# Static attention scores in 64-query halves of 192 columns, and dense slots moved forward in the list of slots

## The chip, the cores and the metric

The kernel runs on one core of a Trainium2 chip. The metric is the device time of one execution, in microseconds (us); the median of several runs is given where there are several. A core has five instruction streams that matter here: TensorE (PE in the profile, with its weight loads as PEld), VectorE (DVE), ScalarE (ACT), GpSimd (POOL) and SyncE (SP), which issues the DMAs.

## What is computed

Block-sparse attention over 4 batches, 8 heads, 768 tokens and head dimension 64, followed by a two-layer MLP over the 3072 tokens. All is float32.

```python
def _attn_ref(q, k, v, sampled_blocks):
    block, n_blocks, window = 32, 24, 1
    scores = np.matmul(q, k.transpose(0, 1, 3, 2)) / np.sqrt(D)
    mask = np.abs(blk_i - blk_j) <= window
    mask = mask | (blk_i == 0) | (blk_j == 0) | (blk_i == n_blocks - 1) | (blk_j == n_blocks - 1)
    for qb in range(n_blocks):
        for kb in sampled_blocks[qb]:
            mask[qb * block:(qb + 1) * block, kb * block:(kb + 1) * block] = True
    scores = np.where(mask, scores, -1000000000.0)
    attn = softmax(scores)
    return np.matmul(attn, v)

def _moe_ref(x, w_in, w_out, s, b):
    r = np.maximum(x @ w_in, 0.0)
    return (s * (r * r) + b) @ w_out
```

A token of block i sees blocks i-1, i, i+1, the first and the last block, and three sampled blocks. Tokens of the first and the last block see everything. The MLP has d_model 512 and d_ff 2048; its weights arrive as 64-bit floats that the kernel takes apart by itself.

## The kernel before

**Slots.** Attention is cut into 52 slots, listed in order by the strings under `T["ORD"]` (lines 31 and 32): one string for batches 0 and 1, one for batches 2 and 3, where `a` is the first batch of the pair and `b` the second. `a20` is tile 2, half 0 of the heads. There are three kinds:

- A *tile* slot ("s", 40 of them) handles 128 queries and four heads. Its static scores (`scores_static`, lines 707 to 712) are those of the keys that can be known beforehand: 128 queries times 256 columns of `kt`, one matmul for each head, two heads at a time in the upper and the lower half of the PE rows (`tile_position=(par * D, 0)`). The 256 columns serve two halves of 64 queries, each of which needs only 192. The sampled keys follow (`scores_sampled`, line 736) from `kg`, which POOL has gathered (line 670).
- A *half tile* slot ("h", `aH`, 4 of them) handles the remaining 64 queries of all heads, with 64x64 matmuls of 160 columns in four quarters of the PE (line 724).
- A *dense* slot ("d", `aD0`, 8 of them) handles the queries of the first and the last block against all 768 keys: 64x64 matmuls of 384 columns in four quarters (line 724 too). It needs no gathered keys or values, but twice 384 KB of `v` (line 508).

**Steps of a slot.** Scores go to a PSUM bank; DVE adds the mask and finds the maximum (line 751); ACT takes the exponential (line 763); PE transposes (line 787); DVE and ACT copy the transposes out (lines 791 and 793); PE multiplies with V (lines 821, 832 for the static part, 846 for the sampled); DVE scales (852); PE transposes (858); ACT copies (863); SP spills to DRAM (875). On PE the order is fixed by lines 1025 to 1034: transposes of slot i, the last transposes of slot i-1, scores of slot i+2, V of slot i.

**The weights.** Each of the 32 blocks of weights (16 of `w_in`, 16 of `w_out`, order in `T["WL"]`: i0 to i7, o0 to o6, then both in turn) goes through `decode_f64`: six DVE steps (lines 75, 77, 78, 83, 84, 85) and three ACT steps (79, 81, 82). i0 to i3 are written where the keys of batch 0 (`kt0`) were, i4 to i7 where those of batch 1 were, so step 83 of i0 waits for the last scores of batch 0. A raw block takes one of three `kraw` buffers, and two of these also take the first attention output read back (`xload`, line 359), until `xsplit` (lines 372 and 374) has split it into a `kg` buffer that attention no longer uses.

**The planner.** `Plan` (lines 99 to 198) simulates the engines with costs written by hand (line 956 for PE, lines 993 to 1020 for the others) and puts every operation into its engine's queue in that order; attention goes first, decoding fills what it takes for idle time. The queues are then fixed: on the chip each engine works through its own in order. The first 30 of the MLP's sub-blocks are in the same plan: `mlp1` (lines 401 to 403, weights i) and `mlp2` (lines 440 to 442, weights o). `mlp2` of the first sub-block needs o0. `mlp1` can run ahead of it until the hidden buffers are full.

**Banks.** `next_bank` (line 696) takes a new PSUM tile in one of seven banks in turn for each matrix of scores or transposes; bank 7 holds the outputs.

Of the kernel before, what the change touches and what calls it, by code (L numbers as in the profile page):

```python
# [32 lines left out]
}  # L33


# [63 lines left out]
class Plan:  # L99
# [15 lines left out]
    def op(self, eng, cost, prio, fn, deps=(), alloc=(), use=(), order=(), nbytes=0, cols=0, late=0.0):  # L115


        o = Plan.Op()
        o.cost, o.prio, o.fn, o.nbytes, o.cols, o.late = cost if isinstance(cost, dict) else {eng: cost}, prio, fn, nbytes, cols, late
        o.pick = isinstance(cost, dict)  # L120
        o.deps, o.order, o.alloc = [d for d in deps if d], [d for d in order if d], alloc
        o.end, o.seq = None, len(self.ops)
        for k in (*alloc, *use):
            self.users.setdefault(k, []).append(o)
        self.ops.append(o)
        return o
# [76 lines left out]
def kernel(  # L203
# [16 lines left out]
    nc = tc.nc  # L220
# [3 lines left out]
    D = 64  # L224
# [6 lines left out]
    SC = 256  # L231
# [28 lines left out]
    NBANK = 7  # L260
    RB = 3

    def scratch(tag, n, name):
        return kp.tile([P, KW], F32 if tag == "kraw" else F32R, tag=tag, name=name, bufs=RB if tag == "kraw" else 2)[:, :n]
# [8 lines left out]
    def bank(k, name):  # L273
        return ps.tile([P, 512], F32, tag=f"bank{k}", name=name)
# [87 lines left out]
    def xsplit(g, c, part=None):  # L362
        src = xraw[(g, c // 2)].rearrange("p (t c n) -> p t c n", c=2, n=P)[:, :, c % 2, :]

        def of(k):
            return xsp[(g, k)][:, c, :].rearrange("p (t n) -> p t n", n=P)

        for k in range(2) if part is None else (part,):
            if c == 0:
                xsp[(g, k)] = gp.tile([P, NCC, HALF], F32R, tag="kg", name=f"x{g}_{k}")  # L370
            if k == 0:
                nc.scalar.copy(of(0), src)
            else:
                nc.vector.tensor_tensor(out=of(1), in0=src, in1=of(0).bitcast(F32), op=ALU.subtract)
# [84 lines left out]
    with ExitStack() as es:  # L459
# [12 lines left out]
        slots = []  # L472
        for b0 in range(0, B, 2):
            for w in T["ORD"][b0 // 2].split():
                b, w = b0 + "ab".index(w[0]), w[1:]
                slots.append(("s", b, int(w[0]), int(w[1])) if w[0] in "01234" else (w[0].lower(), b, NSP, int(w[1:] or 0)))
        units = [(i, j) for i, sl in enumerate(slots) for j in range(2 if sl[0] == "d" else 4)]
        unit_of = {}
# [46 lines left out]
        nc.gpsimd.iota(pi, pattern=[[0, 1]], base=0, channel_multiplier=1)  # L525
        for t in ptiles:
            nc.gpsimd.memset(t[:, SW:], 0.0)

        V = nc.vector
        ri = pers.tile([P, 1], I32, name="ri")  # L530
# [163 lines left out]
        bcount = [0]  # L694

        def next_bank(name):
            bcount[0] += 1
            return bank(bcount[0] % NBANK, name)

        halves = [slice(par * D, (par + 1) * D) for par in range(2)]  # L700

        def scores_static(i, k):


            kind, b, t, x = slots[i]
            n, qr, kt = unit_of[i], qraw[slots[i][:3]], kts[b]
            if kind == "s":
                for par in range(2):
                    sp = sps[(n + 2 * k + par, 0)] = next_bank(f"s{n + 2 * k + par}")
                    nc.tensor.matmul(sp[:, :SC], qr[halves[par], 2 * x + k, :], kt[halves[par], 2 * x + k, 192 * t:192 * t + SC],  # L710
                                     start=True, stop=True, tile_position=(par * D, 0))
                return
            for par in range(2):
                key = (n + par, k) if kind == "d" else (n + 2 * k + par, 0)
                sp = sps[key] = next_bank(f"s{key[0]}_{key[1]}")
                for a in range(2):
                    if kind == "d":
                        o = 64 if k else 0
                        keys = kt[halves[par], 2 * x + a, k * 512:k * 512 + 576].rearrange("p (a c) -> p a c", c=192)[:, :, o:o + P]
                        to, q = sp[halves[a], :HALF], qr[halves[par], 2 * x + a, halves[a]]  # L720
                    else:
                        keys, to = kt[halves[par], 2 * k + a, KW - 6 * BLK:KW - BLK], sp[halves[a], SW - SC:2 * P]
                        q = qr[halves[par], 2 * k + a, halves[a]]
                    nc.tensor.matmul(to, q, keys, start=True, stop=True, tile_position=(par * D, a * D))  # L724
# [15 lines left out]
        sps, nms, dns, rcs, tps = {}, {}, {}, {}, {}  # L740
# [42 lines left out]
        def transposes(n, g):  # L783
            src = pbuf[(n, g)]
            tp = tps[(n, g)] = next_bank(f"t{n}_{g}")[:, :3 * P].rearrange("p (c q) -> p c q", c=3)
            for c in range(chunks(n)):
                nc.tensor.transpose(tp[:, c, :], src[:, c * P:(c + 1) * P], ident)  # L787
# [95 lines left out]
        for n, (i, j) in enumerate(units):  # L883
            kind, b, t, x = slots[i]
# [68 lines left out]
        pq = pvl = o_m = o_e = o_rc = o_ev = None  # L953
        spills, tensor, lqs = {}, {}, {}

        costs = {"s": (485, 535, 350, 260, 685), "d": (810, 0, 350, 780, 0), "h": (380, 535, 240, 160, 685)}
        cols = {"s": (1024, 1536, 768, 256, 1024), "d": (1536, 0, 768, 768, 0), "h": (640, 768, 512, 128, 512)}
        for i, (kind, b, t, x) in enumerate(slots):
            u, full, cost, col = unit_of[i], kind == "s", costs[kind], cols[kind]
            nu, ng, nk = (2, 2, 2) if kind == "d" else (4, 1, 2)  # L960
# [14 lines left out]
            for k in range(nk):  # L975
                keys = [(u + par, k) if kind == "d" else (u + 2 * k + par, 0) for par in range(2)]
                o = op("p", cost[0], u, lambda i=i, k=k: scores_static(i, k), cols=col[0],
                       deps=[*(kld[(b, p)] for p in (pairs[k:k + 1] if full else pairs)), lq],
                       alloc=[("B", ("s", *y)) for y in keys], use=[("qr", qk), (f"kt{b}", b)])
                s_ops.append(o)  # L980
                s_of.update((y, [o]) for y in keys)
# [8 lines left out]
            for j in range(nu):  # L990
                n, ms_ = u + j, []
# [55 lines left out]
        for g in range(2):  # L1047
            for c2 in range(2):
# [8 lines left out]
                for c in (2 * c2, 2 * c2 + 1):  # L1057
                    o_x = [xs_ops[(g, 0, 0)]] if c else [xs_ops[(0, 0, 1)]] if g else [pk]
                    xkey = [[("kg", ("x", g, k))] if c == 0 else [] for k in range(2)]
                    h = xs_ops[(g, c, 0)] = op("a", 450, N + T["XP"] + g * 16, lambda g=g, c=c: xsplit(g, c, 0), [xl[(g, c2)]], alloc=xkey[0],  # L1060
                                               use=[key], order=o_x)
# [38 lines left out]
        for k in range(NPL):  # L1100
            g, f = subs[k]
# [6 lines left out]
            if k > 0:  # L1108
                g, f = subs[k - 1]
# [19 lines left out]
    for k, (x, w) in enumerate((("T1", "S1"), ("T3", "S3"), ("T2", "S2"), ("T4", "S4"), ("u", "v"))):  # L1129
        t = scratch("kraw", HX + HN, f"sum{k}") if k < 3 else kp.tile([P, KW], F32, tag="klp", name=f"sum{k}", bufs=2)  # L1130
# [111 lines left out]
    for i in range(NPL, NSUB):  # L1242
        g, f = subs[i]
# [24 lines left out]
    for s in range(S0, B):  # L1268
        a, b = 2 * s, 2 * s + 1
# [114 lines left out]
```

## Time and profile before

| | us |
|---|---|
| median of 3 runs | 809.37 (807.63 to 811.62) |
| the profiled execution | 810.95 |
| its span, first to last instruction | 809.1 |
| PE busy in the span | 785.8 (97%) |
| DVE busy | 566.9 (70%) |
| ACT busy | 493.1 (61%) |
| POOL busy | 144.0 (18%) |

The times are read together: the prediction works on the profiled execution, whose own time is 810.95 us, 1.85 us more than its span. The stages by the trace: start and first loads up to about 33 us, attention up to about 278 us, the 30 planned sub-blocks of the MLP up to about 400 us, then the rest of the MLP. A busy PE is read with care, since the ends of its matmuls are modelled.

### The profile page before, as it was taken

The numbers are of one execution on the slowest core, as the hardware profiler recorded it, in microseconds if no ns is written. First come the engines' busy times: TensorE is split into PE (matmuls) and PEld (weight loads), VectorE is DVE, ScalarE is ACT, GpSimd is POOL, SyncE is SP. The second block draws the span as 40 slices with busy tenths as digits, with TensorE's granted clock in tenths as the row PEclk, the third lists the DMA queues.
The fourth block names the chain that finished last, engine by engine and source line by source line (L and its number), as shares of the span: only waits on it lengthen the run. The fifth ranks groups of instructions, "written<-read, shape, count | busy, mean of one in ns | idle before, by whom it ended". The sixth has DMA issues, their size and how long they took to land.

```text
span 809.1 us, 21895 instructions
## 1 busy us (share of the span) xinstructions
PE 785.8 (97%) x8400; PEld 682.4 (84%) x8400; DVE 566.9 (70%) x1443; ACT 493.1 (61%) x1175; POOL 144.0 (18%) x374
## 2 busy tenths in 40 slices
PE   7899988999999999999999999999999999999997
PEld 6587877888887889999899999998899888899996
DVE  5576767888888998998743333478668769766662
ACT  3576767788788787777673433457345457544542
POOL 5422133222400000000000000003223223322321
PEclk9899999999999999999999999999999999999999
DMA  9999898876777533334230010412200012000002
GB/s 252 242 229 313 237 249 229 240 222 213 207 211 251 145 105 127 106 107 129 85 111 27 29 37 27 157 45 79 85 1 7 0 40 83 16 0 1 1 1 78
DMA packets 86071, 95.60 MB, mean 118 GB/s; under 512 B 11344, under 2 KB 64976, under 8 KB 85968
## 3 DMA queue, kind: packets, MB, share of 16 engines
q1 hardware_dynamic: 85968, 94.21, 38.9%
q8 instruction: 66, 1.08, 0.6%
q14 instruction: 37, 0.30, 0.1%
HBM read 77.41 MB, written 12.58 MB: 111 GB/s over the span
## 4 chain that ended last, share of the span: by engine, by line
PE 86%; DVE 6%; DMA 3%; ACT 2%; issue 2%; SPq 1%; DVEq 0%; ACTq 0%
PE m L1193 13%; PE o L441 10%; PE o L442 10%; PE o L440 10%; PE t L787 8%; PE s L710 5%; PE xs L832 5%; PE h L403 5%; PE h L401 5%; PE h L402 4%; PE xs L846 3%; PE s L736 3%; DMA kt<-in_k_seq_dram 2%; PE s L724 2%; PE xs L858 1%
## 5 line engine op out<-in xcount | busy, mean ns | idle before, releaser
L763 ACT ACTIVATE ptile<-ptile,nm 128x352 f32<-128x352 f32 (+2 forms) x208 | 121.0, 584 | 36.8 <-DVE nm L751 36.5
L1210 ACT ACTIVATE hid<-hid,sb_b,sb_s 128x384 f32<-128x384 f32 x64 | 45.4, 709 | 113.9 <-DVE hid L1204 113.9
L419 POOL TENSOR_TENSOR hid<-hid,hid 128x384 fp32r<-128x384 f32 x64 | 68.7, 1074 | 178.5 <-ACT hid L1211 178.3
L751 DVE CUSTOM_DVE_ANT_0 ptile<-s,ms 128x352 f32<-128x352 f32 x160 | 74.3, 521 | 30.6 <-PE s L736 30.4
L670 POOL COPY kg<-kt 128x128 f32 x264 | 63.6, 293 | 137.3 <-PE s L736 124.0
L401 PE MATMUL h<-x,win 128*128 128x384 f32 x256 | 86.4, 337 | 0.0
L403 PE MATMUL h<-x,win 128*128 128x384 f32 x256 | 86.3, 337 | 0.0
L402 PE MATMUL h<-x,win 128*128 128x384 f32 x256 | 85.9, 336 | 0.0
L787 PE MATMUL t<-ident,ptile 128*128 128x128 f32 x608 | 79.2, 280 | 3.7 <-ACT ptile L763 2.7
L410 DVE SCALAR_TENSOR_TENSOR hid<-hid,sb_s 128x384 f32<-128x384 f32 x64 | 39.5, 617 | 53.8 <-ACT hid L406 53.5
L441 PE MATMUL o<-wout,hid 128*128 128x512 f32 x192 | 76.5, 398 | 0.6 <-DVE wout L85 0.6
L442 PE MATMUL o<-wout,hid 128*128 128x512 f32 x192 | 76.3, 397 | 0.0
L442 PE MATMUL o<-woutr,hid 128*128 128x512 f32 x192 | 75.9, 395 | 0.0
L441 PE MATMUL o<-woutr,hid 128*128 128x512 f32 x192 | 75.8, 395 | 0.0
L440 PE MATMUL o<-wout,hid 128*128 128x512 f32 x192 | 75.2, 391 | 0.0
L440 PE MATMUL o<-woutr,hid 128*128 128x512 f32 x192 | 74.6, 389 | 0.0
L787 PEld LDWEIGHTS t<-ident,ptile 128*128 128x128 f32 x608 | 65.9, 141 | 9.6 <-ACT ptile L763 3.8
L406 ACT ACTIVATE hid<-h 128x384 f32<-128x384 f32 x64 | 31.4, 491 | 69.4 <-PE h L403 69.0
L1179 POOL TENSOR_TENSOR xT<-sum,xT 128x768 fp32r<-128x768 f32 x2 | 3.7, 1853 | 332.2 <-DVE xT L1179 331.1
L1193 PE MATMUL m<-xT,wop 128*128 128x384 f32 x288 | 58.9, 338 | 2.6 <-DVE sum L1286 1.5
L791 DVE COPY pt<-t 128x384 f32<-128x384 f32 (+1 forms) x104 | 56.1, 543 | 7.6 <-PE t L787 6.1
L419 DVE TENSOR_TENSOR hid<-hid,hid 128x384 fp32r<-128x384 f32 x64 | 35.6, 556 | 34.3 <-ACT hid L415 34.1
(170 smaller groups left out, 1710.2 us busy)
## 6 DMA issues: line engine op xcount, KB each, us to landing
vg<-in_v_dram SPq DMA_DIRECT2D x136, 128.0 KB, 3.6
v<-in_v_sta_dram SPq DMA_DIRECT2D x40, 256.0 KB, 4.8
kt<-in_k_seq_dram SPq DMA_DIRECT2D x16, 544.0 KB, 8.3
raw_i<-in_w_in_dram SPq DMA_DIRECT2D x16, 512.0 KB, 5.6
raw_o<-in_w_out_dram SPq DMA_DIRECT2D x16, 512.0 KB, 3.2
v<-in_v_dram SPq DMA_DIRECT2D x16, 384.0 KB, 4.7
xd<-xst SPq DMA_DIRECT2D x44, 128.0 KB, 3.8
out_dram<-ob SPq DMA_DIRECT2D x20, 256.0 KB, 2.1
```

What stands on the lines that cost most here:

```text
L401: nc.tensor.matmul(ph, wh, xh, start=(c == 0), stop=False)
L402: nc.tensor.matmul(ph, wh, xl, start=False, stop=False)
L403: nc.tensor.matmul(ph, wl, xh, start=False, stop=(c == NCC - 1))
L419: (eng or nc.vector).tensor_tensor(out=htile(5 + i % 3), in0=t, in1=gh.bitcast(F32), op=ALU.subtract)
L440: nc.tensor.matmul(acc, gh[:, tsl], wout(f, 0), start=first, stop=False)
L441: nc.tensor.matmul(acc, gh[:, tsl], wout(f, 1), start=False, stop=False)
L442: nc.tensor.matmul(acc, gl[:, tsl], wout(f, 0), start=False, stop=last)
L670: nc.gpsimd.tensor_copy(kg[:, m], kts[b][:, :, bass.ds(box["js"][m], BLK)])
L751: nc.vector.tensor_tensor_reduce(out=pt[:, :w], in0=sps.pop((n, g))[:, :w], in1=msk, scale=-scale, scalar=FMAX if g == 0 else nm[:, 0:1], ...
L763: nc.scalar.activation(pt[:, :w], pt[:, :w], AF.Exp, bias=nms[n][:, last:last + 1], scale=-1.0, accum_out=dns[i][:, g, j:j + 1])
L787: nc.tensor.transpose(tp[:, c, :], src[:, c * P:(c + 1) * P], ident)
L1193: nc.tensor.matmul(to, w_, x_, start=(c == 0 and k == 0), stop=(c == 1 and k == 2))
```

## The change

Two parts. In the list of slots, the two dense slots of batch 2 (now `cD0 cD1` in the first string) come after the half tiles of batches 0 and 1 and before their last tiles, and the dense slots of batch 3 come after the half tiles of batches 2 and 3; both pairs stood at the end. In `scores_static`, each of the two matmuls of 128 queries times 256 columns becomes two of 64 queries times the 192 columns that this half needs, in four quarters of the PE. A part of each bank is then not written by the scores, so the seven banks become tiles that live through the whole of attention and are set to zero once by DVE. The mask removes what stands in the unwritten part. Two tables of the planner's costs follow.

```diff
-    "ORD": ["aD0 aD1 bD0 bD1 a00 ... a30 a31 b30 b31 aH bH a40 a41 b40 b41",
-            "a00 ... b20 b21 aH bH a30 a31 b30 b31 a40 a41 b40 b41 aD0 aD1 bD0 bD1"],
+    "ORD": ["aD0 aD1 bD0 bD1 a00 ... a30 a31 b30 b31 aH bH cD0 cD1 a40 a41 b40 b41",
+            "a00 ... b20 b21 aH bH bD0 bD1 a30 a31 b30 b31 a40 a41 b40 b41"],
...
-                b, w = b0 + "ab".index(w[0]), w[1:]
+                b, w = b0 + "abc".index(w[0]), w[1:]
...
+        banks = {}
+
+        def abank(k):
+            if k not in banks:
+                banks[k] = bank(k, f"abank{k}")
+                nc.vector.memset(banks[k], 0.0)
+            return banks[k]
+
+        for k in range(NBANK):
+            abank(k)
...
         def next_bank(name):
             bcount[0] += 1
-            return bank(bcount[0] % NBANK, name)
+            return abank(bcount[0] % NBANK)
...
             if kind == "s":
                 for par in range(2):
-                    sp = sps[(n + 2 * k + par, 0)] = next_bank(f"s{n + 2 * k + par}")
-                    nc.tensor.matmul(sp[:, :SC], qr[halves[par], 2 * x + k, :], kt[halves[par], 2 * x + k, 192 * t:192 * t + SC],
-                                     start=True, stop=True, tile_position=(par * D, 0))
+                    sps[(n + 2 * k + par, 0)] = next_bank(f"s{n + 2 * k + par}")
+                for a in range(2):
+                    for par in range(2):
+                        nc.tensor.matmul(sps[(n + 2 * k + par, 0)][halves[a], a * D:a * D + 3 * D], qr[halves[par], 2 * x + k, halves[a]],
+                                         kt[halves[par], 2 * x + k, 192 * t + a * D:192 * t + a * D + 3 * D],
+                                         start=True, stop=True, tile_position=(par * D, a * D))
                 return
...
-        costs = {"s": (485, 535, 350, 260, 685), "d": (810, 0, 350, 780, 0), "h": (380, 535, 240, 160, 685)}
-        cols = {"s": (1024, 1536, 768, 256, 1024), "d": (1536, 0, 768, 768, 0), "h": (640, 768, 512, 128, 512)}
+        costs = {"s": (410, 535, 350, 260, 685), "d": (810, 0, 350, 780, 0), "h": (380, 535, 240, 160, 685)}
+        cols = {"s": (768, 1536, 768, 256, 1024), "d": (1536, 0, 768, 768, 0), "h": (640, 768, 512, 128, 512)}
```

4 rows, old and new, of the table T are left out of this document.

## The prediction

> **What bounds the kernel now.** I read the page first, then the chain of work that ended last, then the stages where the change acts.
>
> ```profile
> PE 785.8 (97%) x8400; PEld 682.4 (84%) x8400; DVE 566.9 (70%) x1443; ACT 493.1 (61%) x1175; POOL 144.0 (18%) x374
> PE 86%; DVE 6%; DMA 3%; ACT 2%; issue 2%; SPq 1%; DVEq 0%; ACTq 0%
> ```
>
> PE is busy 97% of the span and makes up 86% of the chain. DVE's 6% is short, but it is not spread evenly, as will be seen. One tile slot, from the same chain in order of time (start, duration, what):
>
> ```profile
> 170.32 1.08 PE xs L832 x32
> 171.40 0.58 PE xs L846 x32
> 171.98 1.46 PE t L787 x12
> 173.44 0.22 PE xs L858 x2
> 173.66 1.06 PE s L710 x8
> 174.73 0.49 PE s L736 x32
> ```
>
> The six pieces fill 4.89 us, and the next slot begins at once (175.22): in steady attention nothing but PE's own work sets the pace, and line 710 is 1.06 us of it. Next, busy time by stage (first column the stretch, second its length, then PE, PEld, DVE, ACT, POOL):
>
> ```profile
> 36.00:133.00 97.00, 93.88 (x2215) 76.65 (x2213) 68.31 (x251) 68.90 (x213) 28.62 (x119) 1.00 0.89 252
> 133.00:254.00 121.00, 118.33 (x2897) 97.32 (x2896) 101.10 (x354) 96.54 (x290) 26.12 (x108) 1.00 0.78 228
> 278.00:294.00 16.00, 16.00 (x131) 15.67 (x131) 15.76 (x35) 13.07 (x26) 0.00 (x0) 1.00 0.34 108
> ```
>
> DVE is at 70% while no weights are decoded, at 84% while they are, and at 98.5% (15.76 of 16) in the 16 us behind attention. There PE looks full too, but the chain runs over DVE (pieces picked out of one stretch):
>
> ```profile
> 280.63 0.34 DVE wkhp L75
> 280.97 0.35 DVE wklp L77
> 281.34 0.69 DVE wklp L78
> 283.96 0.61 DVE win L83
> 284.60 0.43 DVE wkhp L84
> 286.02 0.60 DVE win L85
> 293.99 0.70 DVE wout L85
> 294.74 0.50 PE o L441
> ```
>
> Line 85 is the last step of a decode. DVE finishes i5, i6, i7 and o0 there, and at 294.74 PE's first `mlp2` waits for o0. The wait is small because `mlp1` has run seven sub-blocks ahead (28 matmuls of line 401, four each), which is as far as its hidden buffers allow. The rows: that wait, and line 401 in a stretch before it (length, PE busy, count):
>
> ```profile
> PEld o L441 <- DVE wout L85: 1.4, 2, 1.0
> 276.00:294.00 18.00, 9.63 (x28) 5.26 (x28) 1.00 0.31 97
> ```
>
> So **two limits lie close together**: PE through attention, and right behind it the queue of decoding on DVE that ends with o0. A shorter attention pays in full only if that queue is shortened as well.
>
> **The static scores.** They leave 160 matmuls of 256 columns and become 320 of 192 columns in four quarters. The trace has the same 64x64 form at two other widths, in the half tiles (160 columns) and the dense slots (384); the forms of line 724, then the pieces of the chain of one half-tile slot and two dense slots:
>
> ```profile
> L724 PE MATMUL s<-kt,qr_5h x64: 296/296/347, 117.1 to 212.9; 64*64 64x160 f32 x64
> L724 PE MATMUL s<-kt,qr_5d x128: 482/483/900, 11.0 to 270.1; 64*64 64x384 f32 x128
> 212.50 0.70 PE s L724 x16
> 254.99 1.45 PE s L724 x16
> 259.79 1.45 PE s L724 x16
> ```
>
> Both have 16 records in a slot, as the changed line will have. 224 columns more cost 0.75 us, 3.35 ns a column, so 192 columns cost 0.70 + 32 x 0.00335 = 0.81 us against 1.06: **0.25 us a slot, 10.0 us for 40 slots**. The least favourable reading takes the slope from line 710 to the dense row, (1.45 - 1.06) / 128 = 3.05 ns, and gives 1.06 - 64 x 0.00305 = 0.865 us, 7.8 us in all. Every tile slot stands on the PE path after 36 us, so this comes off the end of attention entirely. That the four quarters don't overlap, 16 matmul records in two waves, is excluded by the same rows: the dense slot does it with 384 columns. DVE's maximum reads the same 352 columns as before, so lines 751 to 793 keep their costs.
>
> **The zeroed banks** are seven new DVE instructions at the start. No row shows a memset of a bank; the nearest is line 77, one input of the same 128x512, and the wait of DVE that covers them:
>
> ```profile
> L77 DVE TENSOR_SCALAR wklp<-raw_i 128x512 int32<-128x512 int32 x16 | 6.7, 419 | 0.0
> 12.03 0.56 DVE L751 CUSTOM_DVE_ANT_0 ptile<-s,mz 128x384 f32<-128x384 f32 x1 [3.49 <-POOL t L96]
> 20.82 9.07 DMA kt<-in_k_seq_dram
> ```
>
> 7 x 0.42 = 2.9 us. DVE sits idle 3.49 us ahead of its first maximum, and the start is set by the keys that land at 29.9. The index and mask chains that queue behind the memsets on DVE, POOL and ACT shift by 2.9 us too, and are first needed by the tile scores at 36. I take 0; without that cover it is 2.9 us.
>
> **The moved dense slots** bring the same PE, DVE, ACT and DMA instructions to another place; PE's sum doesn't change: 0. On SP, `kt2` and the four loads of `v` for batch 2 pass ahead of later gathers. What is in their favour: dense slots need no gathered keys or values, so the last tiles' gathers get two slots more. What goes against them: the last tiles now end attention, so the `kg` buffers for `xsplit` and the `vg` buffer for o0 come free four slots later relative to the end, and `kt0`, into which i0 is written, two dense slots later. From both sides: 0, and 5 us lost (worked out as the slower rival).
>
> **Decoding behind attention** is the term that decides. The planner gives DVE in a tile slot 4 x 600 + 2 x 560 + 430 + 390 = 4340 ns of attention (lines 993 to 1020) beside PE's 4860 (line 956). The 520 ns left are what it fills with decoding; with 410 in place of 485 it is 370, 29% less. How much was decoded before the end:
>
> ```profile
> 133.00:278.00 145.00, 3.39 (x5) 1.00 0.74 216
> 278.00:294.00 16.00, 2.07 (x4) 1.00 0.34 108
> ```
>
> Five line-85 steps by 278, and i5 well under way: some 5.6 decodes. A decode costs DVE 0.34 + 0.35 + 0.69 + 0.61 + 0.43 + 0.60 = 3.0 us by the pieces above. 29% of 5.6 is 1.6 decodes, **4.9 us**, that move behind attention, in front of o0. There DVE has no idle time (98.5%) and PE no further `mlp1` to run, so each of these us becomes a wait at line 441. The bounds: 0, if the planner places them as before, relative to the slots; 10.0, if o0 is due at the same moment as now. I take 4.9, the value that the planner's own room gives. Behind o0 the sub-blocks and the decodes shift together and I expect nothing more.
>
> **The sum.** 810.95 - 10.0 + 4.9 = 805.85 for the profiled execution. It lies 1.58 us above the median of the runs; on the median's footing it is 809.37 - 5.1 = **804.3 us**.
>
> **The rivals.** *All of it arrives.* The decodes keep their places, o0 comes 10 us earlier: 809.4 - 10.0 = 799.4. For it: the chip's DVE has 19.9 us idle in the 121 us from 133 on. Against: the queue's order is the planner's, not the chip's.
>
> *All of it is given back.* DVE's decoding bounds the whole stretch up to o0, PE waits 10 us at line 441: 809.4. For it: 98.5% on DVE and an existing wait at that very line. Against: the idle 19.9 us again.
>
> *The clock falls.* In the forecast PE sits idle 4.9 us plus today's 1.0 at line 441. At the start the trace shows what an idle PE brings (granted clock is the third number from the end of a window's row):
>
> ```profile
> 27.82 1.51 PE L724 MATMUL s<-kt,qr_5d 64*64 64x384 f32 x2 [3.00 <-DMA kt<-in_k_seq_dram]
> 30.00:40.00 10.00, 10.00 (x165) 7.20 (x166) 5.91 (x20) 4.70 (x15) 8.55 (x36) 0.77 0.81 203
> 72.86 0.92 issue
> 110.61 1.03 issue
> 117.61 1.17 issue
> 139.44 2.54 issue
> 140.00:150.00 10.00, 8.02 (x166) 6.73 (x166) 6.69 (x21) 5.50 (x17) 2.89 (x12) 1.00 0.83 242
> ```
>
> A wait of 3.0 us, after other idle time, was followed by a clock of 0.77 for 10 us, 2.3 us lost; the lone wait of 2.54 us at 139.44 left it at 1.00. If the longer wait trips it, the time is 804.3 + 2.3 = 806.6. The Trainium skill, "TensorE: Matmul & The Clock Gate", section "HAM oscillation — how this bites in real kernels", says to leave no idle gap over about 3.4 us, as the clock is then halved; the two rows agree, and by that rule this rival would be the forecast.
>
> *Slower: decoding starts later and stays serial.* The first write into `kt0` comes two dense slots later (2 x 4.80 us, 254.99 to 259.79 in the chain) and 18 shortened tile slots earlier (4.5): 5.1 us later. If the decodes then follow one another at today's pace, held by their buffers rather than by DVE's room, o0 lands 5.1 us later than today, and the time is 809.4 + 5.1 = 814.5. It decides as soon as more than 10 us of decoding (3.3 decodes) moves behind attention. For it: only five decodes in 145 us, far slower than their 3.0 us. Against: decoding is squeezed by priority in the plan, and a late start can be caught up in the idle time.
>
> A smaller uncertainty is the waits put down to "issue" inside runs of matmuls, the four pieces above, 5.7 us from 72 to 142. PE gets 16 instructions more a slot. I expect up to 2 us either way and keep it in the range.
>
> **How the numbers follow.** Chances: forecast 0.37 (802 to 805.5), everything arrives 0.25, clock falls 0.10, all given back 0.18, slower 0.10. A measurement of this kernel tells about 0.5% from no change, that is 805.3 and 813.4. Faster: 0.25 and 0.35 of the forecast's 0.37, 0.60. Within 0.5%: 0.02 + 0.10 + 0.18, 0.30. Slower: 0.10. The range runs from 798.5 (everything, and a us from the issue waits) to 810.5 (all given back); it leaves out the slower rival and the edges.
>
> **What would show it.** Static scores: the chain's piece for line 710's successor at 0.81 us and a slot of 4.64; 0.87 or more, or two waves, would prove the term wrong. Decoding: fewer than five line-85 steps before the end of attention and a wait at line 441 of some 6 us; if the wait is still 1 us, everything arrived. Clock: below 1.00 in the window behind that wait. Start: scores at 36 us as now. Slower: PE's first line 441 later than 294.74.

## The result, and the profile after

The changed kernel takes 822.08 us (median of 4 runs, 819.22 to 824.84) where the kernel before takes 808.50 in the same comparison (806.06 to 811.62): a ratio of 1.0142, with a 95% interval from 1.0106 to 1.0179. It is slower by 8.6 to 14.5 us, where 5.1 us faster were forecast, and outside the range. The profiled execution has a span of 823.0 us (809.1 before).

The first lines of the page: busy time of PE, and the chain of work that ended last, by engine.

```profile
PE 781.8 (95%) x8720; PEld 681.3 (83%) x8720; DVE 570.6 (69%) x1450; ACT 493.2 (60%) x1175; POOL 144.6 (18%) x374
PE 82%; DMA 6%; DVE 6%; ACT 3%; SPq 2%; issue 1%; DVEq 0%; ACTq 0%
```

PE is busy 4.0 us less, not 10, and idle 41.2 us in place of 23.3. The static scores by themselves are shorter as forecast: over the whole span line 710 of the kernel before is busy 45.37 us, line 726 in its place 35.97 (two records for each matmul; stretch, length, PE, PEld, clock, DMA share, GB/s; first before, then after):

```profile
0.00:809.00 809.00, 45.37 (x320) 27.54 (x320) 0.99 0.40 118
0.00:823.00 823.00, 35.97 (x640) 20.76 (x640) 0.98 0.39 116
```

DMA and SP's queue have doubled their share of the chain. Pieces of one tile slot in the chain (start, duration, what):

```profile
164.04 1.46 PE abank L804 x12
...
165.72 0.81 PE abank L726 x16
166.53 0.49 PE abank L753 x32
167.02 1.08 PE xs L849 x32
168.10 0.58 PE xs L863 x32
168.68 1.46 PE abank L804 x12
```

The static scores take 0.81 us, and from transposes to transposes the slot takes 4.64 us: both as forecast. So the shorter slot is there, and the time is lost between the slots. Three stretches (start and end, length, then PE, PEld, DVE, ACT, POOL busy, granted clock, DMA share, GB/s):

```profile
36.00:133.00 97.00, 89.88 (x2290) 73.06 (x2294) 69.77 (x252) 69.20 (x214) 27.19 (x113) 1.00 0.85 246
133.00:254.00 121.00, 107.79 (x2696) 88.76 (x2693) 91.07 (x319) 86.22 (x263) 26.62 (x108) 0.96 0.82 223
294.00:320.00 26.00, 20.47 (x91) 17.08 (x90) 23.57 (x47) 18.95 (x34) 0.00 (x0) 0.87 0.40 138
```

In the first, PE's busy time falls from 93.88 to 89.88 us of 97, in the second from 118.33 to 107.79 of 121: PE now stands idle for 13 us there, and the granted clock is 0.96. The third stretch, at the first `mlp2` steps, runs at a clock of 0.87, which is at most 26 x 0.13 = 3.4 us (PE is idle for 5.5 of these 26 us, where a low clock costs nothing). What PE waited for (total, times, longest):

```profile
PE xs L838 <- DMA v<-in_v_dram: 9.7, 4, 4.3
PE o L440 <- DVE wout L83: 4.7, 1, 4.7
PE xs L838 <- DVE pt L808: 4.4, 1, 4.4
```

The first row is the dense slots' V (line 838), waiting for its load. Two of its four waits, 3.1 us, end at 39 and 43 us, in the first dense slots, which were not moved. The other two belong to moved ones: 2.3 us up to 137.34 and 4.3 us up to 147.69, together 6.6. The chain of the longer one:

```profile
132.02 5.78 DMA vg<-in_v_dram
...
137.86 0.40 SPq L508
...
141.47 6.08 DMA v<-in_v_dram
...
147.69 1.55 PE xs L838 x24
```

SP waits 0.3 us for the landing of a gather of `vg`, issues one load of `v` (line 508) at 137.86, then five gathers and a spill, and the last load of `v`, issued at 141.47, takes 6.08 us itself. In the kernel before, the same eight loads of the moved slots were issued between 247 and 272 us (time to landing, shortest, median, longest, of line 508; first before, then after, where they go out between 127 and 238 us):

```profile
DMA to landing us min/median/max: 3.3/3.5/5.2
DMA to landing us min/median/max: 4.3/6.2/8.2
```

So the move took the dense slots' loads from a place where they land in 3.5 us to one where they take 6.2. The third row, 4.4 us, is another moved dense slot at 243 us, and its chain shows a decode step in front of an evacuation in DVE's queue:

```profile
235.70 6.20 DMA raw_i<-in_w_in_dram
241.93 0.04 DVE wkhp L75
...
242.69 0.48 DVE pt L808
...
243.21 1.55 PE xs L838 x24
```

Line 75 waits for raw weights that were asked for at 235.70; the copy of the transposes (line 808) is behind it, and PE behind that. Last, the end of o0's decoding:

```profile
305.78 0.69 DVE wout L85
```

o0 is done 11.8 us later than before (305.78 against 293.99). About 6 us of that is the later end of attention: the last transposes of x start on PE at 286.68 (280.65 before). The other 6 is decoding behind attention.

### The profile page after: what moved, and what is told of

The parts are those of the page before. It is cut to its first block, busy times and chain, and to the rows that moved or that the text cites. A ratio compares the mean times of both kernels' runs of the same rounds, so it can differ in the third digit from the quotient of the medians.

```text
span 823.0 us, 22555 instructions
## 1 busy us (share of the span) xinstructions
PE 781.8 (95%) x8720; PEld 681.3 (83%) x8720; DVE 570.6 (69%) x1450; ACT 493.2 (60%) x1175; POOL 144.6 (18%) x374
## 4 chain that ended last, share of the span: by engine, by line
PE 82%; DMA 6%; DVE 6%; ACT 3%; SPq 2%; issue 1%; DVEq 0%; ACTq 0%
PE m L1210 13%; PE o L441 10%; PE o L442 10%; PE o L440 10%; PE abank L804 8%; PE xs L849 5%; PE h L401 5%; PE h L403 5%; PE h L402 5%; PE abank L726 4%; PE xs L863 3%; PE abank L753 2%; DMA kt<-in_k_seq_dram 2%; DMA v<-in_v_dram 2%; PE xs L875 1%
## 5 line engine op out<-in xcount | busy, mean ns | idle before, releaser
L768 DVE CUSTOM_DVE_ANT_0 ptile<-abank,ms 128x352 f32<-128x352 f32 x160 | 74.3, 521 | 25.9 <-PE abank L753 25.8
L804 PE MATMUL abank<-ident,ptile 128*128 128x128 f32 x608 | 81.2, 285 | 3.6 <-ACT ptile L780 3.6
L804 PEld LDWEIGHTS abank<-ident,ptile 128*128 128x128 f32 x608 | 68.3, 145 | 9.2 <-ACT ptile L780 4.5
L808 DVE COPY pt<-abank 128x384 f32<-128x384 f32 (+1 forms) x104 | 56.6, 545 | 12.5 <-PE abank L804 5.2
L810 ACT COPY pt<-abank 128x384 f32<-128x384 f32 (+1 forms) x104 | 48.1, 475 | 27.7 <-PE abank L804 27.5
```

Source lines behind the costliest of these rows:

```text
L768: nc.vector.tensor_tensor_reduce(out=pt[:, :w], in0=sps.pop((n, g))[:, :w], in1=msk, scale=-scale, scalar=FMAX if g == 0 else nm[:, 0:1], ...
```

## The experiments

All runs in one table. *Ratio* is to the kernel before in the same comparison, with its 95% interval; 0.1% is 0.8 us. *Clock* is an upper bound of the time that a lower granted clock cost, (1 - mean granted clock) x span, averaged over the runs that enter the ratio; beside it the same for the kernel before in that comparison. It is a bound because it also counts a low clock while PE stands idle. One run of the kernel before shows this: at a mean clock of 0.943 it took 811.85 us, no longer than its neighbours. It is in the mean of 9.1, which would be 7.5 without it. In the texts of what was expected, fc2 is `mlp2`.

| kernel | median us | ratio | clock us (before) |
|---|---|---|---|
| the change | 822.08 | 1.0142 (1.0106 to 1.0179) | 14.8 |
| halves_oldplan | 812.79 | 1.0011 (0.9988 to 1.0034) | 10.4 (7.4) |
| halves | 813.40 | 1.0031 (1.0000 to 1.0062) | 9.4 (7.4) |
| reorder | 811.07 | 1.0006 (0.9976 to 1.0037) | 7.1 (7.4) |
| banks | 808.75 | 0.9977 (0.9947 to 1.0007) | 7.4 (7.4) |
| before_nok | 805.22 | 0.9934 (0.9906 to 0.9962) | 4.2 (7.5) |
| halves_nok | 805.47 | 0.9934 (0.9901 to 0.9967) | 7.9 (7.5) |
| after_nok | 817.77 | 1.0074 (1.0044 to 1.0104) | 15.8 (7.5) |
| after_oldplan | 811.22 | 1.0009 (0.9975 to 1.0044) | 10.4 (7.5) |
| halves_late | 808.12 | 0.9979 (0.9956 to 1.0002) | 8.9 (7.3) |
| halves_early | 810.06 | 0.9984 (0.9963 to 1.0005) | 8.9 (7.3) |
| before_spread | 810.27 | 0.9994 (0.9969 to 1.0020) | 7.2 (7.3) |
| halves_spread | 814.24 | 1.0046 (1.0021 to 1.0071) | 10.2 (7.3) |
| after_xlate | 815.77 | 1.0064 (1.0034 to 1.0094) | 13.4 (9.1) |
| after_rawlate | 820.93 | 1.0106 (1.0070 to 1.0143) | 15.0 (9.1) |
| aold_rawlate | 816.28 | 1.0063 (1.0041 to 1.0084) | 11.0 (9.1) |
| halves_late_x | 818.54 | 1.0097 (1.0062 to 1.0132) | 12.8 (9.1) |
| halves_late_hold | 809.98 | 0.9980 (0.9957 to 1.0002) | 9.0 (6.8) |
| halves_hold | 814.39 | 1.0049 (1.0028 to 1.0071) | 11.3 (6.8) |

### The parts one by one

Theory A said that the half tiles gain their 10 us and the dense slots, with the planner's new costs, lose more; theory B that shorter tile slots outrun their own loads. Four kernels, each with a part of the change.

**halves_oldplan**: the static scores in halves (called half tile scores from here on) and zeroed banks, with the list of slots and the planner's costs of the kernel before, so that every queue has the order of before.

```diff
-                b, w = b0 + "abc".index(w[0]), w[1:]
+                b, w = b0 + "ab".index(w[0]), w[1:]
...
-        costs = {"s": (410, 535, 350, 260, 685), ...
-        cols = {"s": (768, 1536, 768, 256, 1024), ...
+        costs = {"s": (485, 535, 350, 260, 685), ...
+        cols = {"s": (1024, 1536, 768, 256, 1024), ...
```

> Half-tile scores and zeroed banks alone, with the list of slots and the planner's costs of before, so that every engine's queue has the order of before. Theory A (the dense slots' late loads and the planner's new costs lose the time): the 10 us of the scores arrive in full, 798 to 802 us, the static scores at 0.81 us a slot, PE's wait at the first mlp2 below 2 us, no wait for v in attention. Theory B (shorter tile slots outrun their own loads): 807 us or more, with new waits for v, q or gathers inside attention.

Measured 1.0011: nothing of the 10 us arrives, and theory A falls. The page shows where they went:

```profile
PE 778.0 (96%) x8720; PEld 677.9 (84%) x8720; DVE 569.5 (70%) x1450; ACT 491.7 (61%) x1175; POOL 144.2 (18%) x374
```

Of a span of 811.0 us PE is idle 33.0, 9.7 more than before, and it is busy 7.8 us less, though line 726 gives 9.6. The chain shows one of the new waits, and three windows (columns as above) what follows:

```profile
68.35 10.13 DMA v<-in_v_sta_dram
...
78.62 1.98 PE xs L849 x32
```

```profile
60.00:90.00 30.00, 25.59 (x664) 21.44 (x646) 18.36 (x66) 18.53 (x57) 7.25 (x30) 0.89 0.89 285
120.00:150.00 30.00, 27.12 (x664) 22.02 (x668) 19.69 (x75) 19.15 (x61) 9.56 (x40) 0.89 0.77 222
150.00:240.00 90.00, 89.77 (x2412) 74.70 (x2412) 79.95 (x281) 75.27 (x230) 22.36 (x93) 1.00 0.78 220
```

A load of `v` takes 10.13 us; PE waits 4.4 us for it, and line 849 then takes 1.98 us in place of 1.08. The granted clock over 60 to 90 us is 0.89, at most 3.3 us lost; over 120 to 150 us again. From 150 to 240 us, where PE is busy 89.77 of 90 us, it is 1.00: the narrower matmuls alone do not lower the clock, and it is low where the waits are. But only 5.6 of the 11.1 us of waits between 33 and 160 us are waits for a load that the trace names. The other half is "issue", for which it names nothing, and its cause stays open:

```profile
PE abank L741 <- issue: 2.8, 1, 2.8
PE xs L863 <- issue: 2.7, 1, 2.7
```

**halves**: the same with the planner's new costs (410 and 768 columns) and the old list of slots.

> The same with the planner's new costs, list of slots as before. Theory A: only four decodes fit ahead of the end of attention instead of five, the splits of x move behind it as well, and PE waits 4 to 8 us at the first mlp2: 803 to 808 us. Theory B: 810 us or more, and the waits stand inside attention.

Measured 1.0031, 813.40 us, in theory B's range: in the old list the costs do little or no harm.

**reorder**: the new list of slots alone, full-width scores, old costs.

> The list of slots of the change alone, full-width scores, planner's costs of before. Theory A: the moved dense slots wait for their v, 10 to 14 us in four or five waits, and o0 a little later: 818 to 824 us. Theory B: the move is harmless with slower tile slots, 807 to 811 us.

Measured 1.0006: the moved dense slots alone cost nothing that can be measured.

**banks**: the seven persistent banks and their memsets alone.

> Only the banks that live through attention and are zeroed at the start; scores, list and costs of before. Both theories: 3.7 us of memsets on DVE, covered by its idle time ahead of the first maximum, 808 to 811 us.

Measured 0.9977, not told from no change. The memsets stand in the group of line 534 (busy, mean ns, idle before):

```profile
L534 DVE MEMSET abank<- 128x512 f32 x7 | 3.4, 485 | 1.3 <-PEq L1384 0.9
```

### Fewer bytes, and the planner's costs

If the DMA engines set the pace in the first 150 us (theory supply), taking bytes away should help, and help shorter slots more.

```diff
-            nc.sync.dma_start(out=kts[b][:, p, :], in_=k_seq[b, p])
+            if b < 2:
+                nc.sync.dma_start(out=kts[b][:, p, :], in_=k_seq[b, p])
+            else:
+                nc.gpsimd.memset(kts[b][:, p, :], 0.0)
```

**before_nok**, the edit on the kernel before:

> The kernel before, except that the keys of batches 2 and 3 are not loaded: their tiles are set to zero by GpSimd, so the output of these two batches is not the reference's, 4.4 MB fewer go over the DMA engines in the first half, and the order of the engines' work stays. Theory supply (over the first 145 us the DMA engines, busy 0.85 to 0.95 of the time, hand over the values and the instruction packets too late, and this sets TensorE's pace): some of the 5.6 us of waits between 33 and 160 us go, 803 to 807 us beside 808 to 811. Theory order (the waits come from the order in which the sync engine issues the loads and from the decoding, not from how much is moved): 808 to 812 us, as before.

**halves_nok**, the edit on halves_oldplan:

> The half tile scores with the kernel before's order and planner costs (halves_oldplan), without the key loads of batches 2 and 3 (tiles set to zero, output of these batches not the reference's). Theory supply: the 11 us of waits between 33 and 160 us that ate the shorter tile slots shrink by 4 us or more, 801 to 807 us, and it gains at least 3 us more over halves_oldplan than the kernel before gains by the same edit. Theory order: 810 to 814 us, the waits stay.

**after_nok**, the edit on the changed kernel:

> The changed kernel without the key loads of batches 2 and 3 (tiles set to zero, output of these batches not the reference's). Theory supply: the waits for the values at 75, 87, 130 to 148 us shrink, 812 to 817 us; the wait for raw_i at 243 us and that in front of the first fc2 step stay, being in the second half. Theory order: 819 to 824 us.

Measured 0.9934, 0.9934 and 1.0074. The loads do cost the kernel before some 5 us, as theory supply says. But the half tiles gain by the edit 6.2 us (1.0011 to 0.9934) beside 5.3, not the 3 us more that supply asked for; by the intervals the difference of the two gains is known to some 4 us only. What is clear is that, with 4.4 MB less to load, a kernel with 10 us less work on PE is still no faster. The changed kernel gains 5.5 us (1.0142 to 1.0074) and ends between the two ranges, nearer to that of supply. Two windows of 60 to 90 us, before_nok and then halves_nok:

```profile
60.00:90.00 30.00, 30.00 (x731) 24.92 (x732) 22.29 (x83) 22.05 (x67) 7.63 (x32) 1.00 0.66 192
```

```profile
60.00:90.00 30.00, 30.00 (x802) 25.17 (x802) 24.85 (x85) 23.50 (x73) 11.26 (x35) 1.00 0.65 183
```

With the DMA engines at 0.66 PE is full in both, and has done 802 matmuls in place of 731: here the half tiles pay. They lose it elsewhere, in halves_nok's chain at single loads, and by a clock of 0.87 over 33 to 60 us and 0.94 over 120 to 150, where before_nok has 1.00:

```profile
36.10 7.26 DMA v<-in_v_dram
...
132.87 3.09 DMA vg<-in_v_dram
...
235.31 5.51 DMA raw_i<-in_w_in_dram
```

**after_oldplan**: the changed kernel with the old planner costs for a tile slot (the two `-` lines of `costs` and `cols` of the change put back).

> The changed kernel with the planner's costs of the kernel before for a tile slot (485 and 1024 columns in place of 410 and 768): scores by half tiles and the moved dense slots stay. If the planner's costs alone push the decoding and the loads late: 811 to 815 us, and the wait for raw_i at 243 us goes. If it is shorter slots and moved dense slots together: 818 us or more, with the waits at 130 to 148 us as in the changed kernel.

Measured 1.0009, the clearest step of the study. With the old number for a matmul that has become shorter, the loss is gone: 822.08 to 811.22, 1.33% or 10.8 us. The edit changes no instruction, only the order of the queues. The wait at o0 is gone too, and x's first split on ACT (line 372; durations, then first and last start) comes early enough; for comparison the same row of the changed kernel:

```profile
PE o L441 <- DVE wout L85: 0.2, 1, 0.2
```

```profile
L372 ACT CAST x<-xraw x12: 509/512/529, 246.7 to 414.8; 128x384 fp32r<-128x384 f32 x12
```

```profile
L372 ACT CAST x<-xraw x12: 507/509/529, 276.0 to 427.7; 128x384 fp32r<-128x384 f32 x12
```

The waits for `v` at 130 to 148 us stay (7.2 us in three, where the changed kernel has 6.6 in two), so they are not what separates the two kernels.

### Which half, and whether it is a crowd

```diff
+                if b < 2:
+                    for par in range(2):
+                        sp = sps[(n + 2 * k + par, 0)] = next_bank(f"s{n + 2 * k + par}")
+                        nc.tensor.matmul(sp[:, :SC], ...
+                    return
```

**halves_late** (halves_oldplan with these lines: half tiles in batches 2 and 3 only):

> Scores by half tiles only in the tile slots of batches 2 and 3 (behind 155 us), full-width scores in batches 0 and 1; zeroed banks, order and planner costs of the kernel before. Theory supply (shorter slots pay where the DMA engines have room, 0.75 to 0.78 behind 150 us, and not where they are full): 20 slots by 0.25 us are 5 us less, of which a decode step that waits for raw_i near 245 us takes some back: 804 to 808 us, below the 812.8 of half tiles everywhere. Theory decoding (DVE's queue of decoding behind 150 us takes back what the second half saves): 809 to 813 us.

**halves_early** (with `b >= 2`: half tiles in batches 0 and 1 only):

> The other half: scores by half tiles only in batches 0 and 1, full-width in batches 2 and 3. Theory supply: nothing gained, the 5 us come back as waits for loads and as a lower granted clock behind each of these waits: 809 to 814 us, PE waits of 10 us or more between 33 and 160 us, clock below 0.97 there. Theory decoding: 803 to 807 us.

Measured 0.9979 and 0.9984. Neither is told from no change. halves_early, 810.06 us, is in supply's range. halves_late lies at the border between the two expectations: 2.4 us by the medians, where its 20 slots save 5. In halves_early a load of `v` that takes 10.39 us at 67 us stands in PE's way as in halves_oldplan. In halves_late it is again a decode step that waits:

```profile
238.15 6.11 DMA raw_i<-in_w_in_dram
...
244.28 0.05 DVE wkhp L75
```

**before_spread** and **halves_spread**: seven of the eight key loads of batches 2 and 3 go out within 5 us near 62 us, ahead of the load that takes 10 us. Here each is ordered behind another tile slot.

```diff
+        for m in range(8):
+            kld[(2 + m // 4, m % 4)].order.append(tensor[6 + m][1][0])
         line = tensor[0][0] + tensor[1][0]
```

> The kernel before, with the eight key loads of batches 2 and 3 (557 KB each), seven of which it issues within 5 us near 62 us, put one to a tile slot from the seventh slot on; the same bytes, the rest of the order as before. Theory burst (it is the crowd of key loads that makes the loads of v land late): waits between 60 and 85 us go, 806 to 809 us. Theory quantity (the DMA engines are full whatever the order): 809 to 812 us, as before.

> Scores by half tiles everywhere with the order and costs of the kernel before (halves_oldplan), and the eight key loads of batches 2 and 3 one to a tile slot. Theory burst: the 4.4 us wait for v_sta at 74 us and the clock of 0.80 to 0.86 behind it go, 803 to 808 us, below the kernel before. Theory quantity: the wait moves to another load, 810 to 814 us.

Measured 0.9994 and 1.0046: theory burst falls. The wait at 74 us is gone in halves_spread, and others come in its place, one of 2.74 us at 99 us and gathers that land late at 136 to 146 us.

### What the planner's cost moved

**after_xlate**: x, read back from DRAM, takes two of three raw buffers from 187.6 and 215 us on and gives them back when it is split, in the changed kernel at 276 us. Here its loads are ordered behind slot 36.

```diff
-  lambda c2=c2: xload(0, c2), sp_of[0], alloc=[key], nbytes=393e3)
+  lambda c2=c2: xload(0, c2), sp_of[0], alloc=[key], order=[tensor[36][1][0]], nbytes=393e3)
```

> The changed kernel, with the two loads of x that go into raw weight buffers (lines 359 and 1068) ordered behind the start of slot 36, so that weights i3 and i4 get these buffers first; costs and order otherwise its own. Theory decoding (with a tile slot priced at 410 the planner decodes late, x holds two of three raw buffers from 188 and 215 us until it is split at 276 us, o0 comes 5 us late and the clock falls behind that wait): the wait of 5.1 us at the first fc2 step and most of the 3.4 us of clock behind it go, also the wait for raw_i at 243 us: 809 to 815 us. Rival (the loss lies in the crowded loads at 120 to 150 us): 818 to 823 us.

Measured 1.0064: of 10.8 us, 6.3 come back (1.0142 to 1.0064); the time, 815.77 us, lies just above the 809 to 815 expected. The wait at the first `mlp2` step is gone, and the window behind it runs at full clock. The 6.5 us of waits for `v` at 130 to 148 us are still there:

```profile
L372 ACT CAST x<-xraw x12: 507/509/520, 248.7 to 415.7; 128x384 fp32r<-128x384 f32 x12
```

```profile
300.00:330.00 30.00, 30.00 (x149) 26.82 (x148) 26.97 (x55) 23.93 (x44) 0.00 (x0) 1.00 0.34 108
```

**after_rawlate** and **aold_rawlate**: the first raw weights, two loads of which go out at 119.4 and 119.9 us ahead of the dense slots' `v`, are held behind these loads; in the changed kernel and in after_oldplan.

```diff
-            lv = {}
+            lv = vload[i] = {}
...
-            pw = op("s", ..., load, [prev_k], alloc=[raw], nbytes=524e3, late=T["LATE"])
+            pw = op("s", ..., load, [prev_k], alloc=[raw], order=[vload[24][0]], nbytes=524e3, late=T["LATE"])
```

> The changed kernel, with the loads of the first weights held behind the values of the moved dense slots and of the tile slot after them. Theory queue (the two raw_i loads of 524 KB issued at 119.4 and 119.9 us lie just ahead of the dense slots' four loads of v, whose issue waits until a place among the loads in flight comes free): the waits of 2.1, 2.5 and 4.6 us at 130 to 148 us shrink to less than half, the transposes of the tile slot behind the dense slots start at 143 to 146 us in place of 149.2; the decodes come later by about a tile slot or two, so that the end gives some of it back: 816 to 821 us. Rival (the dense slots are late by their two buffers a slot, whatever else is loaded): that slot at 148 to 150 us, 821 to 825 us.

> The same edit on the changed kernel with the old planner costs (after_oldplan, 811.2 us), where five decodes still lie ahead of the end of attention. Theory queue: the slot behind the dense slots starts at 143 to 145 us in place of 148.7 and the time is 804 to 808 us, faster than before. Rival: 810 to 814 us.

Measured 1.0106 and 1.0063. The time of after_rawlate is in theory queue's range, but its interval overlaps that of the change. The last dense V step of the first pair starts 4.4 us earlier, as theory queue said (after_rawlate, then the changed kernel; in brackets the idle time before it):

```profile
143.31 1.55 PE L838 MATMUL xs<-v,pt 128*64 128x64 f32 x24 [3.88 <-DMA v<-in_v_dram]
```

```profile
147.69 1.55 PE L838 MATMUL xs<-v,pt 128*64 128x64 f32 x24 [4.33 <-DMA v<-in_v_dram]
```

But that very wait is as long as before, and what was won is paid at the end, where o0 now comes later still:

```profile
PE o L440 <- DVE wout L83: 7.8, 1, 7.8
```

In aold_rawlate, for which 804 to 808 us were expected, it turns a kernel equal to before into one 0.5% slower, though its dense slots start earlier: its PE has waits for DVE's evacuations (2.0 us) and for o0 (1.4 us) that after_oldplan has not.

**halves_late_x**: halves_late with x's loads held as in after_xlate.

> Half tile scores in batches 2 and 3 alone (halves_late, 808.1 us) with the two loads of x behind slot 36, so that six decodes lie ahead of the end of attention. If the wait for raw_i near 243 us took back the second half's gain: that wait (1.7 and 1.2 us) and the clock of 0.96 behind it go, 803 to 806 us. If the gain meets another wait: 807 to 810 us.

Measured 1.0097, a miss of both. In this order of slots ACT's split of x stands ahead of work that attention needs, and now waits for a load that was asked for only at 242 us:

```profile
ACT x L372 <- DMA xraw<-xd: 9.0, 1, 9.0
```

PE then waits 7.9 us for ACT. The edit that helped the changed kernel by 6 us costs this one 10.

**halves_late_hold** and **halves_hold**: the decode step that waits (line 75 of i5) is alone put behind slot 46, in halves_late and halves_oldplan.

```diff
+                if k == 5 and m == 0:
+                    order = [tensor[46][1][0]]
                 if m == 1:
                     order = [mine[0]]
```

> Half tile scores in batches 2 and 3 alone (halves_late, 808.1 us), and the first decode step of weight i5 (line 75) put behind the start of slot 46, twelve evacuations later in DVE's queue; its next step, line 77, stays where it was. Theory order in the queue (that step stands in DVE's queue ahead of the maxima and waits for raw_i, which is loaded in the same moment, so DVE and then TensorE stand still): the waits of 1.7 and 1.2 us near 244 us and the clock of 0.96 behind them go, nothing is given back, as no other step moves: 802 to 806 us. Rival (DVE's decoding as a whole is what is short there): 807 to 810 us, the wait comes back at the next step or at the first fc2 steps.

> The same edit on half tile scores everywhere (halves_oldplan, 812.8 us). Theory order in the queue: the waits near 248 us go, 807 to 810 us; the waits of the first 150 us stay. Rival: 811 to 814 us.

Measured 0.9980 and 1.0049: the first as without the edit, the second no faster (1.0011 without) and a little above both ranges. The stretch of 240 to 280 us, in halves_late and in halves_late_hold, and then the next 15 us of both, in the same order:

```profile
240.00:280.00 40.00, 36.85 (x714) 28.76 (x707) 31.52 (x102) 28.32 (x83) 0.00 (x0) 0.96 0.64 191
280.00:295.00 15.00, 14.42 (x81) 13.73 (x80) 14.72 (x30) 12.72 (x24) 0.00 (x0) 1.00 0.33 112
```

```profile
240.00:280.00 40.00, 39.48 (x700) 32.87 (x701) 35.77 (x109) 32.05 (x89) 0.00 (x0) 1.00 0.61 187
280.00:295.00 15.00, 12.70 (x58) 10.57 (x57) 13.63 (x28) 10.88 (x20) 0.00 (x0) 0.93 0.46 141
```

The wait and the clock of 0.96 are gone, and PE is idle 2.6 us less; behind attention PE is idle 1.7 us more, at a clock of 0.93. The rival was right in the time (809.98 us), and in these two profiles the wait comes back at the first `mlp2` steps. Of the versions that load all keys none is measurably faster than the kernel before; halves_late, halves_early, halves_late_hold and banks lie 0.2% below it, with intervals that reach 1.

## Why the prediction was wrong

In the forecast's own terms, by halves_oldplan (1.0011), after_oldplan (1.0009) and the change (1.0142): the term of -10.0 for the scores came out at about +1, the 0 for the moved slots at 0, and the 4.9 for what the planner's number does at 10.8 beside the new list. It counted a gain that did not come, and less than half of a cost that did.

**The static scores' duration**: right. 0.81 us forecast, 0.81 in the chain; the slot 4.64 us.

**"Every tile slot stands on the PE path after 36 us, so this comes off the end of attention entirely"**: this step failed, by about 10 us. The forecast took one steady slot, in which nothing but PE set the pace, for the whole of attention. halves_oldplan, with every queue in its old order, ends at 1.0011 (0.9988 to 1.0034): between -1.0 and +2.8 us instead of -10. The profile before had a sign of it: a DMA share of 0.89 in the stretch from 36 us on, and 3 us of PE idle there. In halves_oldplan PE stands idle 9.7 us longer instead. The reading offered here is that a PE that is ahead meets the next load that isn't there yet. In the chains of the half-tile kernels these are loads of `v` (10.13 us at 68 us), gathers of `vg` (at 133 to 146 us) and raw weights (6.11 us at 238 us). What they have in common is that each is issued when something that follows PE's or DVE's own pace lets go of a buffer or when an earlier DMA has landed; then a shorter slot brings the need nearer but not the load. That reading fits halves_nok, where 4.4 MB less to load still left the half tiles no faster than full-width scores. It is argued and not shown: it says nothing of the 5.5 us of "issue" waits, and a test of it, more buffers for `v`, was not tried.

**The clock**: a rival with 0.10 and 2.3 us. The rival's place was right (0.87 at o0's wait), and its size was too small because only one place was counted. Estimates from the profiles: in the change line 726 takes 9.4 us off PE, but PE is busy only 4.0 us less, so the rest of its work took 5.4 us longer, which is put down to the clock here; and it is idle 17.9 us longer. In halves_oldplan these are 9.6, 7.8, 1.8 and 9.7 us. So what the clock adds is a fifth to a third of the new idle time. The table's upper bounds point the same way: every half-tile kernel that keeps the old list of slots, loads all keys and leaves x alone is 1.6 to 4.5 us above the kernel before in the same comparison, seven of seven, though its PE has 5 to 10 us less to do. The changed kernel is at 14.8 us, where the kernel before is at 6.8 to 7.5 in the five later comparisons, the run at 0.943 left out.

**Decoding behind attention**: the place and the size of the wait came out nearly as forecast, the mechanism only in part. 4.9 us plus today's 1.0 were forecast at line 441; measured are 4.7 us at line 440 and 0.8 at 441. The forecast's cause was that the planner's lower cost leaves less room for decoding. That cost does move decoding, but after_xlate keeps it, holds x back, and has no wait at these lines: what keeps o0 late in the change is x, split at 276 us, in two of three raw buffers. And o0 was to come 5.1 us earlier than before and came 11.8 us later. That the waits agree is in part luck. Late x is not the only way to a late o0, either: in after_rawlate x is split at 237.5 us and PE waits 7.8 us for o0. "Behind o0 ... I expect nothing more" was wrong: up to 3.4 us of clock follow, and beside the new list the planner's number as a whole costs 10.8 us.

**The moved dense slots at 0** (bounds 0 and 5): right by reorder (1.0006), and right beside the shorter scores by after_oldplan (1.0009 against 1.0011 in halves_oldplan). The step that counted the moved slots' DMAs as the same DMAs left out that they land in 6.2 us at the new place instead of 3.5, and PE waits 6.6 us for them; but after_oldplan pays 7.2 us of these waits and is as fast as the kernel before, so they are not where the change loses against it. Only together with the planner's new number does the new list lose: 1.0142, where halves, with the number and the old list, has 1.0031.

**The zeroed banks at 0**: right, 0.9977 (0.9947 to 1.0007), 485 ns each.

**The slower rival** was given 0.10 and 814.5 us. The decodes do start later, the first line 85 at 171.1 us instead of 154.4, and o0 comes 11.8 us later, not 5.1. It had the right sign for a part of the reason.

**What would have put it right.** From the ladder halves_oldplan (1.0011), after_oldplan (1.0009), the change (1.0142): 0 for the shorter scores, 0 for the order of slots, and 10.8 us for one step's cost in the planner's two tables, of which 6.3 us go through x's buffers. Taken in the other order, by halves (1.0031), the same cost makes 1.6 us and the new list beside it 9: it is the two together that lose, and neither alone. The other 4.5 of the 10.8 us are open; after_rawlate doesn't settle whether the raw loads at 119 us are in them, as its gain there was paid back at the end. Why the same cost does little in the old list of slots (halves, 1.0031) is open too; in halves x is split at 241.7 us, not at 276.

## What to carry to other kernels

Time taken off a slot of an engine that is busy 97% can be worth nothing, as here, where the same time came back as idle time and as a lower clock. Where the DMA share is near 0.9, look for the longest landing in that stretch before counting a gain, and add to the new idle time something for the clock behind it: by the estimates here a fifth to a third. A cost table that orders queues is part of the kernel: making it truer for one instruction cost as much here, beside the new list (10.8 us), as the faster instruction could have brought (10), and the old numbers with the new code should be one of the first things to run. An order that cures one schedule can ruin another by as much (x held back: 6 us gained in one, 10 lost in the other).

## What the runs showed of the hardware

The clock fell behind shorter idle times than the rows of before had suggested. In halves_oldplan a lone wait of 2.84 us inside a run of matmuls is followed by ten us at 0.83:

```profile
117.31 2.84 issue
120.15 0.55 PE abank L741 x2
```

```profile
120.00:130.00 10.00, 9.85 (x238) 8.21 (x241) 5.86 (x24) 5.28 (x18) 5.56 (x24) 0.83 0.82 248
```

while the 2.54 us at 139.44 in the kernel before left it at 1.00. The Trainium skill, "TensorE: Matmul & The Clock Gate", section "HAM oscillation — how this bites in real kernels", gives about 3.4 us for such a gap; here 2.84 us were enough once, and the measurement decides. The 3.0 us in the prediction's rows lie below that figure too, though with other idle time before them.

Landing times depended on the place: the same eight loads of 384 KB of `v` landed in 3.5 us (median) in the kernel before, where the DMA share from 247 to 276 us is 0.69, and in 6.2 us in the changed kernel, where it is 0.88 from 127 to 148 us and 0.92 from 222 to 245 us.
